# Retention and MLP in one kernel: q loads in pairs, casts chunk by chunk, rotating PSUM banks, and transposes of q and k moved from TensorE to the DMA crossbar from the eighth chunk on

## The chip, the cores and the metric

The kernel runs on one core of a Trainium2 chip. The metric is the device time of one execution in microseconds (us). Before the change the first three runs had a median of 356.33 us (354.54, 356.33 and an outlier of 1142.12, a first run that nothing here explains). Every kernel below was profiled once and timed in several rounds beside the kernel before, on the same chip.

Words used: a *chunk* is up to 128 rows of one batch (576 rows make four chunks of 128 and one of 64; there are 40). A *block* is 512 rows of the MLP (there are 9). The *issuing queue* is the queue of SyncE, which issues loads, stores and, in the new kernel, the crossbar transposes. The *boundary* is the moment when the first MLP matmul over the third block starts: until then the kernel has to work off chunks and blocks that are all new, after it one stage per block repeats.

## The reference

```python
# q, k, v: [8 batches, 8 heads, 576, 64] float32
scores = scale * q @ k.T                                   # scale = 1/8
gamma  = 1 - 2 ** (-5 - arange(8))                         # one per head
Dmat   = where(rel >= 0, gamma ** rel, 0)                  # rel = query row - key row
x      = ((scores * Dmat) @ v)  # -> [4608, 512], heads side by side
h      = x @ w_in                                          # w_in [512, 2048]
out    = (h * cos(h)) @ w_out                              # w_out [2048, 512]
```

The decay splits into a factor for the key row (put on v, `wv`), one for the query row (put on the output, `up`), and a running state `st` = sum of k^T v over the earlier chunks of the batch. For one chunk the kernel therefore needs k and v with rows on partitions (for the state), and q and k with the head dimension on partitions (for the scores): q and k have to be transposed.

## The kernel before

The program gives each engine a list of instructions of its own. In the trace of the kernel before ScalarE keeps to its order: it evacuates chunk 0 at 16.57 us, after the cast that stands ahead, at 16.03 us, although the transposes were done by 8 us. A small scheduler (`Prog`) notes which tile each instruction reads and writes and inserts the semaphore waits. The parts that the change touches (cuts marked):

```python
def load_chunk(self, g, gate=()):              # three loads, rows of 256 bytes
    b, r, n = CHUNKS[g]
    slot = g % self.NSTG
    for i in (1, 0, 2):                        # k, q, v
        self.P.add("sp", lambda e, i=i: e.dma_start(
            ap(self.STG[slot], 3 * DM, 0, n, i * DM, [D, H], [1, D]),
            bass.AP(self.src[i], (b * H * S + CH * r) * D, [[D, n], [S * D, H], [1, D]])), ...)

def step_t(self, g, ml=None):                  # transposes of q and k on TensorE
    ...
    for i, dst, key in ((1, tk, "tp"), (0, tq, kq)):
        self.P.add("pe", ..., r=[("nat", g % self.NNAT, i), "idn"], w=[key])   # four 128x128 transposes each
    if ml is None:                             # one bank "tp", evacuated by ScalarE
        self.P.add("act", lambda e: e.activation(ap(qk, ...), tk..., AF.Copy), r=["tp"], ...)
        return
    ...

def step_o(self, g, ml=None):                  # the chunk's output goes to the same bank "tp"
    ob, key = (self.T, "tp") if ml is None else (self.ML[ml], ("ml", ml))
    ...

def mlp1(self, lo, hi, f):                     # x @ w_in, cosine on ScalarE, product on VectorE
    i = self.n_ml % 3                          # three banks of its own
    ...

def schedule(self):
    ...
    def T(g):
        if g < NC:
            load_to(g + self.NSTG - 1)         # read-ahead
            cast_to(g + 2)
            self.step_t(g)
    ...
    three = ("act", "dve", "pool")             # q on ScalarE, k on VectorE, v on GpSimd
    load_to(4)
    cast_to(3, three)                          # the casts of chunks 0 to 2 ...
    self.load_win(0, [("stg", 3, 1)])
    self.load_win(1)
    cast_to(4, three)                          # ... and 3 stand before everything else
    ...
    t0(0), self.step_st(0), S_(0)
    for g in (1, 2, 3):
        t0(g), O(g - 1, 3), self.step_st(g), S_(g)
    self.mlp1(0, 256, 0)
    ...
```

## Time and profile before

| Stretch of the kernel before | us | TensorE busy | share of the 16 DMA engines |
|---|---|---|---|
| 0 to 20.9 (loads of four chunks) | 20.9 | 4.98 | 1.09 |
| 57.9 to 96 | 38.1 | 31.69 | 0.97 |
| 97 to 132, one block | 35.0 | 34.31 | 0.76 |
| 132 to 167, one block | 35.0 | 34.16 | 0.54 |

The table is read from the view of windows. Its columns are the stretch and its length, then for each engine the busy time with the number of instructions, then the granted TensorE clock, the mean share of the DMA engines that was busy (the packets' times added up, over the time of 16 engines; it can come out over 1, as in the first line, 1.09) and GB/s.

```profile
core 0: us, PE busy (x) PEld busy (x) DVE busy (x) ACT busy (x) POOL busy (x), PEclk, DMA share, GB/s
0.00:20.90 20.90, 4.98 (x50) 3.43 (x51) 6.73 (x33) 8.37 (x12) 10.28 (x18) 1.00 1.09 183
...
57.90:96.00 38.10, 31.69 (x378) 21.61 (x376) 26.63 (x50) 23.26 (x43) 18.99 (x26) 1.00 0.97 194
97.00:132.00 35.00, 34.31 (x270) 17.57 (x274) 21.51 (x31) 17.26 (x25) 9.71 (x13) 1.00 0.76 154
132.00:167.00 35.00, 34.16 (x251) 17.24 (x254) 19.35 (x29) 17.08 (x25) 8.67 (x12) 1.00 0.54 121
```

From 97 us on TensorE is busy 98% of the two stages shown (94 to 99% of the six up to 308 us), so work taken off TensorE is what can make a stage shorter. Before that it is not: in the first stretch the DMA share is 1.09 and TensorE is busy 5.0 of 20.9 us.

Two lines of the timeline of the kernel before (start, duration, engine, line, output <- inputs, then in brackets the idle time before and what ended it) show the head, a third one the boundary:

```profile
17.20 0.61 PE L256 MATMUL sc<-qk 64*128 64x128 bf16 x8 [8.86 <-ACT qk L242]
...
26.45 0.61 PE L339 MATMUL ml<-xt,win 128*128 128x256 bf16 x4
...
96.85 0.81 PE L339 MATMUL ml<-xt,win 128*128 128x512 bf16 x3 [0.16 <-issue]
```

Chunk 0 is transposed by 8 us, but its scores (L256) start at 17.2 us, because ScalarE has the casts of chunks 1 to 3 ahead of the evacuation (L242) in its list, and the last of those waits for its load. The first MLP matmul starts at 26.45 us. (The clock column needs care here: the first clock record in this trace is at 25.4 us, and a 1.00 before it only means that there is none. Groups of scores last 0.61 us up to 23.4 us and 0.40 us at 26.1 us.)

What a transpose costs TensorE is read from the starts of neighbours in the timeline of the kernel before, in a full stage:

```profile
160.04 0.61 PE L229 MATMUL tp<-idn,nat 128*128 128x128 bf16 x8
160.48 1.03 PE L339 MATMUL ml<-xt,win 128*128 128x512 bf16 x4
```

The eight transposes of a full chunk hold the stream for 0.44 us (the 0.61 us is the modelled end of a pipelined group).

### The profile page before, as it was taken

Reading aid. Unit: us, or ns where it says so; the run is one execution under the profiler, and the core shown is the slowest. Engines: PE = TensorE matmul, PEld = TensorE weight load, DVE = VectorE, ACT = ScalarE, POOL = GpSimd, SP = SyncE. Lnnn points to the kernel's source line nnn. Section 1 sums busy time; section 2 is a strip of 40 time slices with the busy share of each in tenths; the row PEclk is TensorE's granted clock in tenths of the full one; section 3 lists DMA queues with packets and bytes.
Section 4 is the critical chain, followed back from the end, with each engine's and each line's share of the span. In section 5 each row is a group of like instructions: output and inputs, shape, how many; then the busy total and the mean of one; then the engine's idle time right before and its main releaser. Section 6 shows DMA issues by size and latency. Waiting matters only on the chain.

```text
span 352.5 us, 6098 instructions
## 1 busy us (share of the span) xinstructions
PE 318.1 (90%) x2428; PEld 166.9 (47%) x2464; DVE 189.0 (54%) x307; ACT 165.7 (47%) x252; POOL 90.7 (26%) x128
## 2 busy tenths in 40 slices
PE   1098989788899999999999999999999899999997
PEld 1064334555555544545454545445554444444444
DVE  2287713587865754555555655555646555433300
ACT  6235712656646434454455444544454444344421
POOL 2530544266623222402332222313331000000000
PEclk9999999999999999999999999999999999999999
DMA  9999996799999525555259525555200000110012
GB/s 177 183 204 186 187 198 133 197 221 205 208 203 208 126 76 119 121 119 121 74 121 207 122 74 122 120 121 119 76 30 32 30 32 30 51 40 31 32 60 89
DMA packets 122091, 42.33 MB, mean 120 GB/s; under 512 B 113232, under 2 KB 117584, under 8 KB 122064
## 3 DMA queue, kind: packets, MB, share of 16 engines
q1 hardware_dynamic: 117840, 37.76, 49.5%
q0 software_dynamic: 4224, 4.19, 7.4%
q8 instruction: 19, 0.31, 0.4%
q14 instruction: 8, 0.07, 0.1%
HBM read 36.70 MB, written 9.44 MB: 131 GB/s over the span
## 4 chain that ended last, share of the span: by engine, by line
PE 82%; DVE 6%; ACT 5%; SPq 3%; issue 2%; DMA 1%; DVEq 0%
PE ml L358 35%; PE ml L339 34%; PE tp L229 4%; PE sc L256 3%; PE tp L309 3%; SPq L185 3%; ACT cb L346 2%; DVE gt L349 2%; DVE pt L264 2%; ACT qk L237 2%; PE tp L299 2%; PE st L276 2%; DMA stg<-in_q_dram 1%; DVE xt L319 1%; PE ml L309 1%
## 5 line engine op out<-in xcount | busy, mean ns | idle before, releaser
L349 DVE TENSOR_TENSOR gt<-ml,cb 128x512 bf16<-128x512 f32 (+3 forms) x164 | 102.4, 625 | 120.9 <-ACT cb L346 96.4
L346 ACT ACTIVATE cb<-ml,cpi 128x512 bf16<-128x512 f32 (+3 forms) x164 | 103.8, 635 | 125.9 <-PE ml L339 125.6
L339 PE MATMUL ml<-xt,win 128*128 128x512 bf16 (+3 forms) x632 | 145.4, 353 | 5.8 <-DVE xt L319 2.4
L358 PE MATMUL ml<-wout,gt 128*128 128x512 bf16 (+1 forms) x580 | 142.1, 374 | 1.7 <-ACT os L371 0.7
L339 PEld LDWEIGHTS ml<-xt,win 128*128 128x128 bf16 x656 | 57.2, 98 | 57.8 <-DVE xt L319 3.1
L358 PEld LDWEIGHTS ml<-wout,gt 128*128 128x128 bf16 x592 | 53.9, 98 | 59.0 <-ACT os L371 3.1
L212 POOL CAST nat<-stg 128x512 bf16<-128x512 f32 (+1 forms) x72 | 42.6, 612 | 122.1 <-PE st L276 108.9
L214 POOL TENSOR_TENSOR nat<-stg,wv 128x512 bf16<-128x512 f32 (+1 forms) x40 | 41.7, 1043 | 38.1 <-DMA stg<-in_v_dram 16.4
L264 DVE TENSOR_TENSOR pt<-sc,tri 128x1024 bf16<-128x1024 f32 (+1 forms) x40 | 44.3, 1107 | 8.9 <-PE sc L256 8.9
L237 ACT ACTIVATE qk<-tp 128x1024 bf16<-128x1024 bf16 (+1 forms) x36 | 33.3, 926 | 13.4 <-PE tp L229 13.3
L371 ACT ACTIVATE os<-ml 128x512 f32<-128x512 f32 (+1 forms) x37 | 21.7, 586 | 29.9 <-PE ml L358 29.6
L229 PE MATMUL tp<-idn,nat 128*128 128x128 bf16 (+1 forms) x304 | 22.7, 218 | 4.5 <-DVE nat L212 4.5
L256 PE MATMUL sc<-qk 64*128 64x128 bf16 (+1 forms) x320 | 15.8, 221 | 10.3 <-ACT qk L242 8.9
L319 DVE TENSOR_TENSOR xt<-tp,up 128x512 bf16<-128x512 f32 (+1 forms) x36 | 22.5, 624 | 4.0 <-PE tp L309 3.8
L229 PEld LDWEIGHTS tp<-idn,nat 128*128 128x128 bf16 (+1 forms) x304 | 18.4, 99 | 12.9 <-DVE nat L212 4.5
L285 DVE TENSOR_TENSOR sbd<-st,bdm 128x512 bf16<-128x512 f32 x32 | 21.8, 680 | 0.0
L256 PEld LDWEIGHTS sc<-qk 64*128 64x128 bf16 (+1 forms) x320 | 9.2, 99 | 24.1 <-issue 13.0
L299 PE MATMUL tp<-qk,sbd 128*128 128x128 bf16 (+1 forms) x116 | 10.4, 212 | 5.1 <-ACT qk L237 2.9
L309 PE MATMUL tp<-pt,nat 128*64 128x128 bf16 (+1 forms) x288 | 14.1, 219 | 0.8 <-ACT qk L237 0.7
L299 PEld LDWEIGHTS tp<-qk,sbd 128*128 128x128 bf16 x116 | 8.0, 97 | 12.0 <-DVE pt L264 3.0
L276 PE MATMUL st<-nat 128*128 128x128 bf16 x128 | 13.1, 228 | 0.0
L276 PEld LDWEIGHTS st<-nat 128*128 128x128 bf16 x128 | 9.9, 101 | 5.7 <-issue 0.3
(35 smaller groups left out, 46.4 us busy)
## 6 DMA issues: line engine op xcount, KB each, us to landing
out_dram<-os SPq DMA_DIRECT2D x35, 256.0 KB, 2.1
stg<-in_k_dram SPq DMA_DIRECT2D x32, 256.0 KB, 4.4
stg<-in_q_dram SPq DMA_DIRECT2D x32, 256.0 KB, 4.9
stg<-in_v_dram SPq DMA_DIRECT2D x32, 256.0 KB, 4.8
win<-in_moe_w_in_dram POOLq DMA_DIRECT2D x4, 512.0 KB, 7.4
wout<-in_moe_w_out_dram POOLq DMA_DIRECT2D x4, 512.0 KB, 11.5
stg<-in_k_dram SPq DMA_DIRECT2D x8, 128.0 KB, 3.7
stg<-in_q_dram SPq DMA_DIRECT2D x8, 128.0 KB, 3.6
```

The lines of the kernel that those rows point to most:

```text
L212: fn = lambda e, dst=dst, src=src: e.tensor_copy(dst, src)
L214: self.P.add(engs[2], lambda e: e.tensor_tensor(ap(nat, 3 * DM, 0, n, 2 * DM, [D, H], [1, D]), ap(stg, 3 * DM, 0, n, 2 * DM, [D, H], [1, D ...
L229: inst = e.transpose(dst[:, c * 128:c * 128 + n], ap(na, 3 * DM, 0, n, i * DM + 128 * c, [1, 128]), ap(self.IDN, 128, 0, n, 0, [1, n]))
L237: self.P.add("act", lambda e: e.activation(ap(qk, 1024, 0, 128, 0, [128, 8], [1, n]), tk.rearrange("p (c n) -> p c n", c=8)[:, :, 0:n], AF ...
L256: inst = e.matmul(ap(self.SC, 1024, 0, n, hp * 512 + c * 128, [1, n]), ap(qk, 1024, 64 * hp, 64, c * 128, [1, n]), ap(qk, 1024, 64 * hp, 6 ...
L264: self.P.add("dve", lambda e: e.tensor_tensor(ap(pt, 1024, 0, n, 0, [128, 8], [1, n]), ap(self.SC, 1024, 0, n, 0, [128, 8], [1, n]), ap(se ...
L276: inst = e.matmul(ap(self.ST, 512, 0, 128, c * 128, [1, 128]), ap(na, 3 * DM, 0, n, DM + c * 128, [1, 128]), ap(na, 3 * DM, 0, n, 2 * DM + ...
L309: inst = e.matmul(ap(ob, 512, 64 * hp, 64, c * 128, [1, n]), ap(na, 3 * DM, 0, n, 2 * DM + (2 * c + hp) * D, [1, D]), ap(pt, 1024, 0, n, h ...
L339: inst = e.matmul(ap(ps, 512, 0, 128, 0, [1, n]), ap(self.WIN, 4 * DFF, 0, 128, c * DFF + 128 * f, [1, 128]), ap(self.XT, 4 * TOK, 0, 128, ...
L346: self.P.add("act", lambda e: e.activation(ap(cb, TB, 0, 128, 0, [1, n]), ap(ps, 512, 0, 128, 0, [1, n]), AF.Sin, bias=self.CPI.ap(), scal ...
L349: self.P.add("dve", lambda e: e.tensor_tensor(ap(gt, NF * TB, 0, 128, f * TB + lo - TB * j, [1, n]), ap(ps, 512, 0, 128, 0, [1, n]), ap(cb ...
L358: return e.matmul(ap(ps, 512, 0, 128, 0, [1, cn]), ap(gt, NF * TB, 0, 128, f * TB + 128 * t, [1, 128]), ap(self.WOUT, NF * DM, 0, 128, f * ...
```

## The change

Its intent: take the transposes off TensorE where TensorE is the limit, and start earlier. In detail:

- **Crossbar.** From chunk 7 on (`BYPE`) the cast q and k are transposed by a DMA from SBUF to SBUF, two chunks ahead (`LEAD`), and issued in the queue that also loads and stores. Chunks 0 to 6 stay on TensorE.
- **Paired q.** q is loaded for two chunks at once in rows of 512 bytes (two neighbouring rows per partition). The queries of a chunk then lie as even rows, odd rows; mask, `up` and the output pattern are permuted to match.
- **Banks.** One bank stays with the second MLP matmul, four rotate over everything else (`bank()`), instead of three for the MLP and one "tp".
- **Head.** The casts of a chunk stand right before its work, and warm-up matmuls on zeros run before and between the first chunks. Chunks 4 to 8 are asked for after the third output weight (before: chunks 4 and 5 after the first, the others later).

The core of the diff, cut:

```diff
-    def step_t(self, g, ml=None):
+    def bank(self, hold=False):
+        while self.turn % 5 in self.held:
+            self.turn += 1
+        i = self.turn % 5
+        self.turn += 1
+        ...
+        return i, self.BK[i], ("bk", i)
...
+    def load_q(self, d, gate=()):
+        b, r = d // 3, d % 3
+        n, slot = (128, 128, 32)[r], d % self.NQ
+        self.P.add("sp", lambda e: e.dma_start(
+            ap(self.QSTG[slot], 2 * DM, 0, n, 0, [2 * D, H], [1, 2 * D]),
+            bass.AP(self.src[0], (b * H * S + 256 * r) * D, [[2 * D, n], [S * D, H], [1, 2 * D]])),
+            r=list(gate), w=[("qstg", slot)], sem=f"q{slot}")
...
+    def move_k(self, g):
+        n, k, t = CHUNKS[g][2], g % self.NNAT, g % self.NKT
+        self.P.add("sp", lambda e: e.dma_start_transpose(
+            ap(self.KT[t], DM, 0, 128, 0, [128, 4], [1, n]), ap(self.NAT[k], 2 * DM, 0, n, 0, [1, DM])),
+            r=[("nat", k, 0)], w=[("kt", t)], sem=f"kt{t}")
+
+    def move_q(self, d):
+        ...  # the same for a pair: QT <- QNAT, eight 128x128 blocks
...
+        BYPE, LEAD = 7, 2
...
         def T(g):
-            if g < NC:
-                load_to(g + self.NSTG - 1)
-                cast_to(g + 2)
-                self.step_t(g)
+            if g >= NC:
+                return
+            load_to(g + LEAD + 4)
+            cast_to(g + LEAD + 2)
+            if g < BYPE:
+                if pair(g):
+                    self.step_tq(dbl(g))
+                self.step_tk(g)
+            x = g + LEAD
+            if BYPE <= x < NC:
+                if pair(x):
+                    self.move_q(dbl(x))
+                self.move_k(x)
...
         load_to(4)
-        cast_to(3, three)
...
+        warm(10)
+        for g in range(4):
+            self.cast_k(g, "act")
+            if g % 2 == 0:
+                self.cast_q(g // 2, ("act", "dve"))
+            self.cast_v(g, "pool")
+            if g == 2:
+                self.load_win(0, [("stg", 3, 0)])
+                self.load_win(1)
+            self.step_tk(g)
+            if g % 2 == 0:
+                self.step_tq(g // 2, "dve")
+            if g:
+                self.step_o(g - 1)
+            self.step_s(g)
+            self.step_st(g)
+            if g < 3:
+                warm(2)
         self.load_win(2)
         self.load_win(3)
...
+        load_to(9, [("wout", 2)])
```

## The prediction

> What bounds the kernel now. From 97 us to the end TensorE is the limit: in each stretch of 35 us (one per block of 512 tokens) it is busy 34.3 us, and its waits from 97 to 308 us add up to 4.3 us. Before that it is not. The first MLP matmul starts at 26.4 us (timeline): the casts of chunks 1 to 3 stand before the evacuation of chunk 0 in ScalarE's order, so chunk 0's scores wait 9.1 us and start at 17.2 us. From 50 to 100 us TensorE is idle 8.5 us, waiting for the one bank "tp", its evacuation and the score mask, while the DMA share is about 1.0 until 120 us.
>
> What the change does.
> 1. TensorE loses the transposes of 33 of 40 chunks. In the timeline eight transposes take 0.45 us (0.34 us for a 64-row chunk): 26 x 0.45 + 7 x 0.34 = 14 us, all on the critical path; 11 us of it after 97 us.
> 2. ScalarE loses most of 33 us of evacuations; at 47% busy this is worth little.
> 3. Head: casts by chunk and warm-up matmuls let chunks 0 to 3 be worked off as they land. The last loads land no later (a 256-byte packet takes 21 ns, 1 KB 47 ns; I estimate 28 ns for the paired 512 bytes). The first MLP matmul should start near 21 us, limited by the first weights, 5.5 us after their issue at 15 us. Gain 5 us.
> 4. Rotating banks and transposes done ahead remove most TensorE waits between 50 and 97 us. But chunks 4 to 8 are asked for later (after the third output weight), so the first block's second matmuls should wait for weights (36 to 41 us) and chunks 5 to 7 for loads. DMA paces 36 to 85 us. What stands at 97 us now should stand near 87.
> 5. Added: 33 k moves (128 KB) and the q pairs (256 KB) through the crossbar, in order on the queue that loads and stores. The trace has no such transfer. [...] The loads cost 3.6 us per chunk and stores 0.7, so it fits, with two chunks (15 us) of lead.
> 6. Strided masks and outputs on VectorE: same element counts, no change (1.22 and 0.69 us).
>
> Sum: 354.5 - 10 (until 97 us) - 11 (after) = about 334 us. Range 325 to 349. Faster by over 2%: 0.80; within 2%: 0.09; slower: 0.11.
>
> What would show it. Right: a block's stage falls from 35 to about 33 us; TensorE stays over 96% busy there; about 60 transposes remain; first MLP matmul at 20 to 22 us; crossbar moves land within 6 us and TensorE hardly waits for kt or qt. Wrong: the issuing queue busy throughout, matmuls of "sc" waiting for kt or qt, stages over 36 us; or weight waits in the first block eating the head's gain.
>
> What would make it wrong. Crossbar moves slow or exclusive with other DMAs: above 3 us per chunk the early phase, with its full DMA, slips first; [...]. Gains could be larger if the early phase is less tied to DMA than I think.

Two passages are cut from the prediction, where marked: what point 5 gave for the cost of a move, figures and an estimate that no trace of this case showed, and in the last paragraph a threshold for the whole kernel that followed from them. The sum came to 333.5, about 334 us, and loses no term: the moves had none in it, because the prediction let them fit beside loads and stores. By the numbers, two chunks are 15 us, and 7.5 us less 3.6 for loads and 0.7 for stores leaves 3.2 us of a chunk for moves, about the 3 us of the last paragraph.

## The result, and the profile after

The changed kernel gives the right result and took 341.42 us in the median of four runs (341.2 to 343.32), against 356.22 us before. Ratios in this document are the mean time of one kernel's fast runs over that of the other's of the same rounds, so they are not quite the ratio of the medians: here 0.9611, with a 95% interval of 0.9558 to 0.9665. The kernel is faster.

| | before | after | predicted |
|---|---|---|---|
| first MLP matmul, us | 26.45 | 20.89 | near 21 |
| first matmul of the second MLP half, us | 43.34 | 35.92 | waits for weights, 36 to 41 |
| boundary, us | 96.85 | 96.10 | near 87 |
| boundary to the end, us | 255.7 | 243.3 | about 245 (11 less) |
| span of the profiled run, us | 352.5 | 339.4 | |

So 12.4 us of the 13.1 us lie after the boundary. (The medians differ by 14.8 us; the profiled run of the kernel before, 354.54 us, was the fastest of its four.) The head came 5.6 us earlier, as predicted, and by the boundary all but 0.75 us of that was lost again.

The view of windows of the changed kernel, in the stretches that answer to those above:

```profile
0.00:20.90 20.90, 15.60 (x128) 9.02 (x129) 11.31 (x38) 10.98 (x17) 10.33 (x19) 0.76 0.99 181
...
57.90:96.00 38.10, 26.75 (x274) 18.88 (x274) 25.57 (x51) 15.01 (x33) 18.74 (x26) 0.82 1.07 203
96.00:129.00 33.00, 32.58 (x227) 15.67 (x230) 20.76 (x29) 12.79 (x19) 15.17 (x22) 1.00 1.13 215
129.00:162.00 33.00, 32.44 (x221) 15.48 (x224) 19.50 (x29) 13.56 (x21) 9.47 (x14) 1.00 0.66 155
```

A stage is now 33 us with TensorE busy 98 to 99% of it. Between 57.9 and 96 us TensorE is busy only 26.75 us of 38.1, at a lower clock (0.82), while the DMA share is 1.07. Where it stands is seen in TensorE's timeline of the changed kernel:

```profile
20.89 0.61 PE L393 MATMUL bk<-xt,win 128*128 128x256 bf16 x4
...
39.98 1.89 PE L415 MATMUL bk<-wout,gt 128*128 128x512 bf16 x8 [1.30 <-DMA wout<-in_moe_w_out_dram]
...
46.29 0.62 PE L279 MATMUL bk<-idn,qnat 128*128 128x128 bf16 x8 [1.32 <-POOL qnat L222]
...
64.47 0.61 PE L315 MATMUL sc<-qt,kt 64*128 64x128 bf16 x8 [6.54 <-DMA kt<-nat]
65.01 3.38 PE L393 MATMUL bk<-xt,win 128*128 128x320 bf16 x12
...
81.19 0.40 PE L315 MATMUL sc<-qt,kt 64*128 64x128 bf16 x8 [1.55 <-DMA kt<-nat]
...
90.23 0.40 PE L315 MATMUL sc<-qt,kt 64*128 64x128 bf16 x8 [1.88 <-DMA kt<-nat]
...
96.10 0.81 PE L393 MATMUL bk<-xt,win 128*128 128x512 bf16 x3 [0.16 <-issue]
```

The scores of chunk 7, the first chunk whose k comes through the crossbar, wait 6.54 us. Later ones wait 1.55 and 1.88 us. The long wait costs more than its length: after it the granted clock is about half. A view of finer windows of the changed kernel shows it:

```profile
57.90:64.50 6.60, 0.06 (x4) 0.03 (x4) 0.72 (x1) 0.10 (x1) 5.50 (x8) 0.66 0.97 196
64.50:69.70 5.20, 5.20 (x29) 3.15 (x30) 2.85 (x5) 1.58 (x3) 1.65 (x2) 0.50 1.06 240
69.70:80.00 10.30, 9.94 (x105) 6.41 (x103) 9.50 (x19) 6.66 (x13) 4.44 (x6) 0.97 1.13 217
...
90.50:94.40 3.90, 3.90 (x39) 3.44 (x34) 3.05 (x6) 1.68 (x4) 0.61 (x1) 0.56 1.45 166
```

At a clock of 0.50 for 5.2 us, TensorE does what would take 2.6 us at full clock, so by this estimate the wait of 6.5 us costs about 9 us. The last line shows a clock of 0.56 also after a gap of 1.88 us, in a stretch where TensorE had stood several times (busy 2.69 us of the 5 from 85 to 90 us). After the gap of 1.55 us, from 81.2 to 85 us, the clock was 1.00. Which gap brings the clock down is not shown.

Why kt came late is seen in the timeline of the issuing queue (SPq, what was issued and for how long it held the queue):

```profile
51.27 1.06 SPq L433 DMA_DIRECT2D out_dram<-os  x1
52.37 0.60 SPq L192 DMA_DIRECT2D stg<-in_k_dram  x1
53.02 0.64 SPq L200 DMA_DIRECT2D qstg<-in_q_dram  x1
53.71 0.60 SPq L192 DMA_DIRECT2D stg<-in_v_dram  x1
54.35 1.51 SPq L192 DMA_DIRECT2D stg<-in_k_dram  x1
55.91 1.14 SPq L200 DMA_DIRECT2D qstg<-in_q_dram  x1
57.09 1.83 SPq L192 DMA_DIRECT2D stg<-in_v_dram  x1
58.96 2.89 SPq L296 DMA_TRANSPOSE qt<-qnat  x1
61.90 1.26 SPq L290 DMA_TRANSPOSE kt<-nat  x1
```

GpSimd had cast q and k of chunk 7 by 52.8 us. Their moves went out at 58.96 and 61.90 us, behind a store and the loads of chunks 9 and 10. The queue is busy without a gap (none over 0.12 us between two issues) from 37 to 104 us. Between 60 and 96 us, 19.4 us of the 36 are moves (durations of L290 and L296 in the timeline, cut at the ends of the stretch) and 13.3 us are loads.

The list of DMA issues of the changed kernel gives the time from issue to landing (median, us):

```profile
kt<-nat SPq DMA_TRANSPOSE x33, 3.0
qt<-qnat SPq DMA_TRANSPOSE x20, 5.1
```

### The profile page after: what moved, and what is told of

The parts are those of the page before. It is cut to its first block, busy times and chain, and to the rows that moved or that the text cites. A ratio compares the mean times of both kernels' runs of the same rounds, so it can differ in the third digit from the quotient of the medians.

```text
span 339.4 us, 5764 instructions
## 1 busy us (share of the span) xinstructions
PE 311.9 (92%) x2184; PEld 158.8 (47%) x2220; DVE 189.8 (56%) x304; ACT 139.7 (41%) x223; POOL 96.3 (28%) x137
## 3 DMA queue, kind: packets, MB, share of 16 engines
q1 hardware_dynamic: 131056, 45.50, 63.9%
## 4 chain that ended last, share of the span: by engine, by line
PE 70%; DMA 14%; SPq 6%; POOL 3%; issue 2%; DVE 2%; ACT 1%; DVEq 0%; POOLq 0%
PE bk L415 33%; PE bk L393 30%; DMA wout<-in_moe_w_out_dram 5%; DMA qstg<-in_q_dram 5%; DMA kt<-nat 4%; SPq L192 3%; PE sc L315 2%; PE bk L364 2%; DMA stg<-in_k_dram 2%; PE st L334 1%; PE bk L356 1%; POOL win L206 1%; DVE gt L403 1%; SPq L290 1%; SPq L200 1%
## 5 line engine op out<-in xcount | busy, mean ns | idle before, releaser
L400 ACT ACTIVATE cb<-bk,cpi 128x512 bf16<-128x512 f32 (+3 forms) x164 | 103.8, 635 | 151.3 <-PE bk L393 150.3
L403 DVE TENSOR_TENSOR gt<-bk,cb 128x512 bf16<-128x512 f32 (+3 forms) x164 | 101.8, 625 | 100.0 <-ACT cb L400 97.5
L393 PE MATMUL bk<-xt,win 128*128 128x512 bf16 (+3 forms) x640 | 147.5, 360 | 3.0 <-issue 1.3
L415 PE MATMUL bk<-wout,gt 128*128 128x512 bf16 (+1 forms) x573 | 142.1, 373 | 3.4 <-DMA wout<-in_moe_w_out_dram 1.3
L415 PEld LDWEIGHTS bk<-wout,gt 128*128 128x128 bf16 x592 | 55.3, 98 | 65.0 <-ACT os L430 3.7
L393 PEld LDWEIGHTS bk<-xt,win 128*128 128x128 bf16 x656 | 59.4, 100 | 54.7 <-DVE xt L374 2.1
L222 POOL CAST nat<-stg 128x512 bf16<-128x512 f32 (+1 forms) x36 | 21.9, 609 | 110.5 <-DMA stg<-in_k_dram 93.0
L430 ACT ACTIVATE os<-bk 128x512 f32<-128x512 f32 (+1 forms) x37 | 21.7, 586 | 29.9 <-PE bk L415 29.9
L374 DVE TENSOR_TENSOR xt<-bk,up 128x512 bf16<-128x512 f32 (+1 forms) x40 | 26.7, 668 | 6.8 <-PE bk L364 6.7
L222 POOL CAST qnat<-qstg 128x512 bf16<-128x512 f32 (+1 forms) x44 | 25.8, 612 | 16.4 <-DMA qstg<-in_q_dram 15.4
L315 PE MATMUL sc<-qt,kt 64*128 64x128 bf16 (+1 forms) x320 | 16.1, 223 | 11.8 <-DMA kt<-nat 10.6
```

The source lines that it names most:

```text
L222: self.P.add(eng, lambda e: e.tensor_copy(dst, src), r=r, w=w)
L315: inst = e.matmul(ap(self.SC, 1024, 0, n, hp * 512 + c * 128, [1, n]), ap(kt, DM, 64 * hp, 64, c * 128, [1, n]), self.queries(g, 64 * hp, ...
L374: self.P.add("dve", lambda e: e.tensor_tensor(ap(self.XT, 4 * TOK, 0, 128, b * S + CH * r, [TOK, 4], [1, 2], [2, h]), ap(ob, 512, 0, 128, ...
L393: inst = e.matmul(ap(ps, 512, 0, 128, 0, [1, n]), ap(self.WIN, 4 * DFF, 0, 128, c * DFF + 128 * f, [1, 128]), ap(self.XT, 4 * TOK, 0, 128, ...
L400: self.P.add("act", lambda e: e.activation(ap(cb, TB, 0, 128, 0, [1, n]), ap(ps, 512, 0, 128, 0, [1, n]), AF.Sin, bias=self.CPI.ap(), scal ...
L403: self.P.add("dve", lambda e: e.tensor_tensor(ap(gt, NF * TB, 0, 128, f * TB + lo - TB * j, [1, n]), ap(ps, 512, 0, 128, 0, [1, n]), ap(cb ...
```

## The experiments

Two theories for the lost early gain, and what each says:

- **Q, the queue's order**: moves stand behind loads that nobody needs yet. Put in front, or with the loads elsewhere, the waits go.
- **B, the traffic**: until about 100 us the DMA path is full; every packet and every issue added there costs, whoever waits for it.

The gain after the boundary needed a test too: transposes off TensorE, or banks? Twelve kernels were run. All gave a right result. The boundary is read from one profile per run: four runs that are nearly the same up to that point (e2_pe13, e3_nocross, e5_pe13_order and e11_double, all with chunks 0 to 12 on TensorE) have it at 88.55, 90.52, 91.21 and 90.34 us, so it is good to about 1.5 us. Medians and ratios are firmer.

| run | edit | median us | ratio to before (95%) | boundary us |
|---|---|---|---|---|
| the change | | 341.42 | 0.9611 (0.956 to 0.967) | 96.1 |
| e1_order | moves ahead of loads | 339.37 | 0.9573 (0.954 to 0.961) | 92.4 |
| e2_pe13 | TensorE transposes chunks 0 to 12 | 334.56 | 0.9427 (0.938 to 0.948) | 88.6 |
| e3_nocross | TensorE transposes all | 347.14 | 0.9778 (0.974 to 0.982) | 90.5 |
| e4_nowarm | no warm-up matmuls | 341.67 | 0.9625 (0.959 to 0.966) | 96.9 |
| e5_pe13_order | e2 and e1 | 335.59 | 0.9430 (0.939 to 0.947) | 91.2 |
| e6_pe10_order | chunks 0 to 9, and e1 | 334.82 | 0.9414 (0.938 to 0.944) | 88.3 |
| e7_q256 | q in 256-byte rows | 347.14 | 0.9771 (0.974 to 0.980) | 101.1 |
| e8_ghost | e2, moves of 7 to 12 kept unused | 343.12 | 0.9654 (0.963 to 0.968) | 95.1 |
| e9_kv_by_act | k, v loads by ScalarE from chunk 4 | 365.22 | 1.0293 (1.026 to 1.033) | 119.0 |
| e10_late_att | e6, attention of 4 to 6 later | 334.84 | 0.9427 (0.939 to 0.946) | 87.1 |
| e11_double | e5, moves twice from chunk 16 | 334.69 | 0.9420 (0.937 to 0.947) | 90.3 |
| e12_kv_by_act9 | k, v loads by ScalarE from chunk 9 | 346.94 | 0.9754 (0.972 to 0.979) | 99.8 |

### e1_order: moves ahead of loads

```diff
         def T(g):
             ...
-            load_to(g + LEAD + 4)
-            cast_to(g + LEAD + 2)
-            if g < BYPE: ...
+            cast_to(g + LEAD + 1)             # what is moved has to be cast
             x = g + LEAD
             if BYPE <= x < NC:
                 ...
+            load_to(g + LEAD + 4)
+            cast_to(g + LEAD + 2)
+            if g < BYPE: ...
```

> Only the order in the issuing queue changes: the crossbar moves of a chunk go out ahead of the loads of a chunk three further on. Theory Q (in the early phase the moves stand in the queue behind loads that are not needed yet): the wait of 6.5 us of the scores for kt at 58 us falls below 2 us, the boundary to the third block (first 512-column matmul, 96.1 us in the changed kernel) comes 5 to 8 us earlier, total 333 to 337 us. Theory B (the 16 DMA engines are full until then and any order pays the same bytes): the waits move from kt to the casts and loads, the boundary moves by less than 2 us, total 339.5 to 342.

Measured: 339.37 us, ratio 0.9573; the intervals of this run and of the changed kernel overlap. The first wait went, and a later one, at chunk 10, came in its place. The timeline of TensorE in e1_order:

```profile
60.70 0.40 PE L315 MATMUL sc<-qt,kt 64*128 64x128 bf16 x8 [0.23 <-DMA kt<-nat]
...
77.55 0.44 PE L315 MATMUL sc<-qt,kt 64*128 64x128 bf16 x8 [3.78 <-DMA kt<-nat]
```

The measured boundary (3.7 us earlier) and total lie between the two expectations. Order decides which chunk waits. By the medians it is worth 2 us of the total, which is not clear of the noise.

### e2_pe13: TensorE keeps the transposes of chunks 0 to 12

```diff
-        BYPE, LEAD = 7, 2
+        BYPE, LEAD = 13, 2
```

> TensorE keeps the transposes of chunks 0 to 12 (changed kernel: 0 to 6); the crossbar starts only when the early phase is nearly over. Costs TensorE 6 x 0.40 = 2.4 us of matmuls, takes some 11 us of DMA engine time (1.8 us a chunk, estimated from the packets) off the phase 50 to 96 us. Theories Q and B both expect the boundary at 96.1 us to come earlier, by 5 to 8 us, total 333 to 337. If neither the queue order nor the DMA time of the moves is the limit (the loads themselves, or the weights, are), the boundary stays within 2 us and the total is 340 to 343.

Measured: 334.56 us, ratio 0.9427, clear of the changed kernel's interval. The boundary comes 7.5 us earlier although TensorE does more work before it (5.9 us earlier if the mean of the four like profiles, 90.2 us, is taken), and the part after it takes the same 243 us (331.8 - 88.55). No scores wait for kt before the boundary. The line of the boundary in the timeline of e2_pe13:

```profile
88.55 0.81 PE L393 MATMUL bk<-xt,win 128*128 128x512 bf16 x3 [0.67 <-DVE gt L403]
```

So the early moves are what took most of the early gain.

### e3_nocross: no crossbar at all

```diff
-        BYPE, LEAD = 7, 2
+        BYPE, LEAD = 40, 2
```

> No crossbar at all: TensorE transposes every chunk, everything else of the change stays. If the gain after 96 us is the transposes taken off TensorE, a block's stage goes back from 33.2 to about 35 us and the part after the boundary from 243 to about 254 us. If the early phase lost its gain to the moves, the boundary comes to 88 to 91 us. Together 342 to 346 us. If the steady gain came from the banks instead, the stage stays near 33 us and the total is near 333.

Measured: 347.14 us, a little above the range; boundary 90.5 us as expected; from there to the end 256.4 us, as in the kernel before (255.7). A stage of e3_nocross in the view of windows:

```profile
125.50:160.50 35.00, 34.18 (x254) 17.16 (x256) 19.59 (x28) 17.27 (x27) 9.46 (x14) 1.00 0.46 117
```

The stage is back at 35 us. The whole gain after the boundary comes from the transposes taken off TensorE, and rotating banks alone give none there. From the first MLP matmul to the boundary e3_nocross takes 69.6 us, the kernel before 70.4: banks, casts and paired q together are worth little there too (0.8 us, within what the boundary scatters).

### e4_nowarm: no warm-up matmuls

```diff
-        warm(10)
...
-            if g < 3:
-                warm(2)
```

> The warm-up matmuls on zeros are left out. If the early start comes from the casts by chunk alone, the first MLP matmul stays at 20.5 to 21.5 us and the total within 1 us of 341.4. If the warm-up keeps TensorE's clock up, the first MLP matmul comes 1.5 us or more later and the total is 342.5 or more. In the trace the attention matmuls between 9.6 and 19 us take 0.61 us a group, as in the kernel before, so I expect the first.

Measured: 341.67 us, first MLP matmul at 20.75 us. The first expectation held: the warm-up does nothing measurable for the total here. Only the first two groups of transposes, at 7.6 and 8.1 us, are faster in the changed kernel (0.40 and 0.62 us against 0.61 and 1.03), and not in every run with the warm-up (0.61 and 1.03 us in e9_kv_by_act). Why it does not last is not shown: TensorE stood 1.9 us before the first of them and 0.9 us before the scores at 9.6 us, and from 10 to 15 us, busy 4.66 us of 5, it was granted a clock of 0.50. The timeline of the changed kernel has a group of scores at 0.61 us as late as 17.6 us, and the first at 0.40 us after 20 us. So the earlier start comes from the rest of the new head. The paired q load has a part in it: with rows of 256 bytes (e7_q256, below) the first MLP matmul starts at 22.27 us, 1.4 us later. The remaining 4 us are put down to the casts by chunk; no run takes them apart from the banks.

### e7_q256: the paired q load in rows of 256 bytes

```diff
     def load_q(self, d, gate=()):
-        self.P.add("sp", lambda e: e.dma_start(
-            ap(self.QSTG[slot], 2 * DM, 0, n, 0, [2 * D, H], [1, 2 * D]), ...
+        for x in range(2):
+            self.P.add("sp", lambda e, x=x: e.dma_start(
+                ap(self.QSTG[slot], 2 * DM, 0, n, x * D, [2 * D, H], [1, D]), ...
```

> The changed kernel, but each paired q load of 512-byte rows is split into two loads of 256-byte rows into the same places: same bytes, twice the packets, one more issue per pair. From the packet times (30.7 ns for 512 bytes, 22.2 for 256) a pair costs 0.9 us more of the 16 engines and about 0.6 us more of the issuing queue, so some 8 us for the 9 pairs asked for before the boundary. If DMA time paces the early phase (theory B), the boundary at 96.1 us comes 4 to 8 us later and the total is 345 to 350. If only the order of the queue mattered (theory Q), it moves by less than 2 us, total 340 to 343. After the boundary no change in either.

Measured: 347.14 us, boundary 101.1 us, 5.0 us later. This is what theory B expects, and far from Q. 1.4 us of the 5.0 are lost before the first MLP matmul. Same bytes, twice the packets and issues: the early phase has no room for the two together; the run does not part them. From the packet records of the changed kernel, the 16 engines spend 35.4 us on q with 512-byte rows (18,432 packets of 30.7 ns over 16), and would spend by estimate 51 us with 256-byte rows (twice the packets at 22.2 ns, the mean of its packets of 256 bytes, over 16).

### e8_ghost: the early moves issued, but nobody waits for them

```diff
-        BYPE, LEAD = 7, 2
+        BYPE, LEAD = 13, 2
...
             x = g + LEAD
+            if 7 <= x < BYPE:                 # into tiles that nothing reads
+                if pair(x):
+                    self.ghost_q(dbl(x))
+                self.ghost_k(x)
```

> As the run in which TensorE transposes chunks 0 to 12 (334.6 us, boundary at 88.6), but the crossbar moves of chunks 7 to 12 are issued as well, at the places where the changed kernel has them, into tiles that nothing reads: their traffic and their time in the queue stay, only nobody waits for their result. If their traffic delays the loads and casts by itself (theory B), the boundary goes back to 93 us or later and the total to 339 or more. If the loss was the latency of the result, late behind loads (theory Q), the boundary stays at 88 to 91 and the total at 334 to 337.

Measured: 343.12 us, boundary 95.1 us: theory B's numbers. The timeline of TensorE in e8_ghost shows chunk 7 not waiting, and the first chunk that does use a move, chunk 13, waiting for all of it:

```profile
61.04 0.40 PE L329 MATMUL sc<-qt,kt 64*128 64x128 bf16 x8
...
94.18 0.61 PE L329 MATMUL sc<-qt,kt 64*128 64x128 bf16 x8 [5.02 <-DMA kt<-nat]
```

Chunks 7 to 12 themselves were not slowed: up to 88 us the run keeps the pace of e3_nocross. Chunk 13's k was cast by 78.3 us, but its move was issued only at 90.37 us, behind loads and ghost moves (79.19 us in e2_pe13). So the time that the early moves take is lost even when nobody waits for them, and it is felt at the first move that is used. What this doesn't part is the moves' traffic from the time that they hold the queue. (The list of the queue's waits puts 4.6 us, in two waits, on a ghost move of q, L310, and names a cast of k. That move doesn't read k; the casts that it reads had ended at 53.1 and 74.6 us, before the moves came up at 58.3 and 84.6 us. The named releaser is not the cause.)

### e5_pe13_order and e6_pe10_order: both edits; and fewer chunks on TensorE

```diff
-        BYPE, LEAD = 7, 2
+        BYPE, LEAD = 13, 2      # e6_pe10_order: 10, 2;  both with the order of e1_order
```

> Both edits that helped: TensorE transposes chunks 0 to 12, and later moves go ahead of the loads in the queue. If the order only matters while the moves lie in the full early phase, this adds nothing to the first edit: total 333.5 to 335.5, boundary at 88 to 89. If moves behind loads still cost something later, it gains up to 2 us more.

> TensorE transposes chunks 0 to 9, moves ahead of loads. Three chunks less on TensorE than with 13: 1.2 us of matmuls saved, three chunks' moves (5 us of the engines) back in the full phase. If the DMA time is what counts, the boundary is 1 to 3 us later than with 13 and the total 335 to 337; if only the first moves, just after the weights, are the trouble, the total is 333 to 334.5.

Measured: 335.59 and 334.82 us, ratios 0.9430 and 0.9414, not to be told from e2_pe13 (0.9427). Once the early moves are gone, order adds nothing (335.59 is 0.1 us above the range given, and the boundary of 91.2 us is 2 us later than expected, within what the boundary scatters). With moves in front, starting with chunk 10 is as good as with chunk 13. Its 334.82 us lie between the two ranges given, its boundary of 88.3 us beside the best. Runs with the same order show where the trouble lies: e1_order has the moves of chunks 7 to 9 in addition and is 4.6 us slower, while e5_pe13_order lacks those of chunks 10 to 12 and is no faster. So the trouble comes with the first moves, right after the weights, and not with every move before 96 us. Whether chunk 10 does as well without the new order was not run.

### e9_kv_by_act and e12_kv_by_act9: k and v loads from another queue

```diff
     def load_kv(self, g, i, gate=()):
-        self.P.add("sp", lambda e: e.dma_start(
+        self.P.add("act" if g >= 4 else "sp", lambda e: e.dma_start(      # e12_kv_by_act9: g >= 9
```

> The changed kernel, but from chunk 4 on the k and v loads are issued by ScalarE instead of the issuing queue; the same transfers, the same bytes, moves and stores stay where they are and no longer stand behind these loads. Takes 1.2 us of issuing per chunk (0.6 us a load) from a queue that is busy without a gap from 37 to 104 us. If that queue is the limit of the early phase (its order or its issue time; theory Q), the waits for kt go, the boundary comes from 96.1 to 88 to 91 us, total 333 to 337. If the 16 DMA engines are the limit (theory B), the boundary stays at 94 to 98, total 339 to 344. Risk for both: ScalarE's cosines wait behind its loads, which would show as TensorE waiting for ScalarE or VectorE.

Measured: 365.22 us. The run is faulty as a test: ScalarE also had to issue loads gated by the third output weight. It stood until that had landed, then issued ten loads from 37.5 us on, at a DMA share of 0.9 or more (the slices from 36.3 to 54.5 us on its page), and did nothing else until 51.9 us. The list of waits of e9_kv_by_act (from 20 to 100 us) has it in one line:

```profile
ACT L400 <- issue: 32.3, 1, 32.3
```

The next run mends this.

> The run before, without its fault: there ScalarE also had to issue the gated loads of chunks 4 to 8 and stood still until the third output weight had landed (31 us). Here ScalarE issues the k and v loads from chunk 9 on only; chunks 4 to 8, all moves and all stores stay in the issuing queue, the bytes are the same. If the queue (order or issue time) makes the moves late, the waits for kt of 6.5, 1.6 and 1.9 us go and the boundary comes from 96.1 to 88 to 91 us, total 333 to 337 us. If the 16 engines' time alone does, the boundary stays at 94 to 98 us and the total at 339 to 344. In between (91 to 94): both.

Measured: 346.94 us, boundary 99.8 us: slower than the changed kernel, and outside both ranges. TensorE's timeline of e12_kv_by_act9:

```profile
69.44 0.61 PE L315 MATMUL sc<-qt,kt 64*128 64x128 bf16 x8 [8.12 <-DMA kt<-nat]
```

The first wait grew from 6.5 to 8.1 us. ScalarE now asked for chunks 9 and 10 at 42 to 48 us, ahead of chunks 7 and 8, whose loads then held the issuing queue 2.0 to 3.3 us each (1.1 to 1.7 us in the changed kernel). This speaks against the strong form of theory Q, that loads only block moves in the queue: loads taken out of the queue still cost. But they were also asked for earlier than in the changed kernel. The later waits for kt did go, and waits of TensorE for VectorE came (1.3 us at the boundary), so the run does not cleanly split engine time from issue time.

### e11_double: every move twice, from chunk 16 on

```diff
                 self.move_k(x)
+                if x >= 16:
+                    if pair(x):
+                        self.ghost_q(dbl(x))
+                    self.ghost_k(x)
```

> As the run with TensorE transposing chunks 0 to 12 and moves ahead of loads (335.6 us), but from chunk 16 on every move is issued twice, the second time into tiles that nothing reads. If the moves are free wherever the DMA engines have room (share 0.6 to 0.86 in the stages after the boundary; the doubling adds some 1.8 us a chunk, 0.25 of a stage), the total stays within 1.5 us, 334 to 337, and a stage at 33 us. If the issuing queue or the crossbar is near its limit there too, scores wait for kt again and the total is over 340.

Measured: 334.69 us. A stage of e11_double in the view of windows:

```profile
157.00:190.00 33.00, 32.59 (x234) 15.56 (x236) 21.00 (x30) 13.16 (x20) 10.51 (x15) 1.00 1.01 204
```

The DMA share rises to 1.01 and the stage stays at 33 us. After the boundary the moves are free, even twice.

### e10_late_att: fill the waits for chunks 4 and 5 with other work

```diff
-        run(m[:4], [])
+        run(m[:8], [])
...
-        run(m[4:], att)
+        run(m[8:], att)
```

> As the run with TensorE transposing chunks 0 to 9 and moves ahead of loads (334.8 us), with the attention of chunks 4 to 6 started after eight quarters of the first block's second matmuls instead of four, so that TensorE does not stand waiting for chunk 4 and 5 (waits of 0.75 and 2.1 us in the trace). If those waits are idle time that other work can fill, 2 to 3 us are gained: total 331.5 to 333.5. If the loads pace the phase anyway, the waits move to chunks 6 to 9 and the total is 334 to 336.

Measured: 334.84 us against 334.82 for e6_pe10_order. The waits for chunks 4 and 5 fell to 0.4 us, and waits for kt came at chunks 10, 12 and 13 (0.5, 1.4 and 0.9 us in its timeline). The total is the one of the second expectation; the waits moved to the crossbar moves and not to the loads of chunks 6 to 9. Shifting work does not help here.

The experiments give a version that beats both kernels: the changed kernel with `BYPE` at 13 (334.56 us), or at 10 with moves ahead of loads (334.82 us). They are equal within the noise.

## Why the prediction was right or wrong

The total (334 us, range 325 to 349) was forecast as faster, and 341.42 us lies in the range. The mechanism was mostly right, and one term of the sum was mis-sized.

- **Transposes off TensorE (point 1), right.** Predicted 11 us after the boundary; measured 12.4 us (255.7 to 243.3). A stage fell from 35 to 33 us as said, and e3_nocross shows that it takes the crossbar: without it the stage is back at 35 us.
- **ScalarE (point 2), not tested apart.** It lost 26 us of busy time (165.7 to 139.7 us, 47 to 41% of the span). The 2 us of a stage are about the transposes taken off TensorE (4.4 chunks of 0.44 us), which leaves nothing for ScalarE to explain.
- **Head (point 3), right.** First MLP matmul predicted near 21 us, measured 20.89. But the warm-up had no part in it (e4_nowarm).
- **Weights and loads after the head (point 4), right in kind.** TensorE waited 1.3 us for the output weights and 1.3 us for the cast of chunk 5, between 36 and 47 us.
- **"What stands at 97 us now should stand near 87" (point 4), wrong in size.** It stood at 96.1: 0.75 us in place of 10. This is the term that failed, and most of it is the early moves: with none before chunk 13 the boundary stood at 90.2 us (mean of four), 6 us earlier. The other 3 us belong to "Rotating banks and transposes done ahead remove most TensorE waits between 50 and 97 us": about 5 us were forecast for it, and from the first MLP matmul to the boundary those four runs took 69.3 us in the mean, against 70.4 us before. The prediction did say that crossbar moves would let "the early phase, with its full DMA," slip first, but above 3 us per chunk; below that it let them fit.
- **The moves' cost and "so it fits" (point 5), wrong before the boundary.** In packet time, shared out over the 16 engines, the moves cost at most 1.8 us a chunk: the packets of the hardware queue took 63.9% of 339.4 us in the changed kernel and 45.6% of 346.9 us in e3_nocross, 58.7 us more, over 33 chunks. This includes what they slow the other packets. At 7.74 MB more (45.50 against 37.76) that is 132 GB/s, while the loads of the kernel before in rows of 256 bytes (28.3 MB, 110,592 packets of 21.1 ns over 16 engines, 145.6 us) moved 194 GB/s. In the issuing queue a k move (128 KB) holds 1.27 us and a q pair (256 KB) 2.03 us in the median, so some 2.3 us for a full chunk. Both are under the 3.2 us that the numbers of the prediction leave. What was wrong was the time it compared them with, that of a chunk after the boundary (7.5 us in its lead of 15 us for two). Before the boundary chunks 7 to 12 pass in about 5 us each (64.5 to 95.5 us for six), the queue is never idle, and by then it has also asked for chunks up to 17, ahead of need. There the same 2 us do not fit. They pile up as a wait at the first chunk that uses a move, and the clock drop after it (0.50 for 5.2 us) adds to the bill. The prediction had itself listed these signs under "Wrong", and they came in the early phase: the issuing queue without a gap from 37 to 104 us, and matmuls of "sc" waiting for kt, 10.6 us in all, every one of these waits before 96.1 us. A full DMA share alone is not enough: from 96 to 129 us it is 1.13, and no scores wait.

That the early moves cost, whoever waits for them, is shown by e2_pe13 (away: 6 to 7.5 us earlier) and e8_ghost (kept but unused: back at 95.1); e7_q256 (more packets and issues in the same order: 5.0 us later) shows that it is not only their place in the queue. That place in the queue matters a little is suggested by e1_order. Left open: how much of the backlog is time of the 16 engines and how much issue time of the queue, since both are full there (a DMA share of 1.07 from 57.9 to 96 us, a queue without a gap) and e12_kv_by_act9 changed both; and whether a shorter read-ahead of loads, or moves issued from another queue, would let the early moves fit, which no run tried.

## What to carry to other kernels

Moving work from a full engine to a path with room pays only where the path has room: look at that path in each stage, not over the whole span. Its busy share alone does not decide (moves were free in stages with a share of 1.01 and 1.13); compare what the path needs for one chunk with the time that a chunk has there (here about 5 us before the boundary and 7.4 us after, 33 us over the 40/9 chunks of a block), and switch the move on where it fits. When a new transfer costs time in a full queue, issue it without using its result: if the time stays lost, as it did here, waiting for the result was not the cause. Look for the loss at the next transfer that is used. Count with a wait on TensorE the matmuls at a lower clock that follow it: here 5.2 us at 0.50 after the wait of 6.54 us.
